# A column of ones beside v, first v loads from GpSimd, scores ahead of transposes, and two weight pieces a step at the end

## The chip, the cores and the metric

The kernel runs on one NeuronCore of a Trainium2 chip. The metric is the time of one execution on the device in microseconds (us), as the median of the runs; lower is better. The engines are called by the names of the profile: PE (TensorE), DVE (VectorE), ACT (ScalarE), POOL (GpSimd) and SP (SyncE, which here only issues DMAs).

## What is computed

Eight batches of attention in chunks of 64 tokens are followed by a Fourier mixing layer and a two-layer perceptron.

```python
# q, k, v: (8, 8 heads, 576, 64) float32; 9 chunks of 64 tokens; each attends within itself
scores = scale * q_c @ k_c^T
attn = exp(scores - max(scores)); attn = attn / (sum(attn) + 1e-9)
x = (attn @ v_c)  ->  (8, 576, 512)
# Fourier mixing and the perceptron
u = x + real(fft(fft(x, axis=1), axis=2))
un = (u - mean(u)) / sqrt(var(u) + 1e-6)
out = u + relu(un @ w_ch1) @ w_ch2      # w_ch1 (512, 2048), w_ch2 (2048, 512), given as float64
```

## The kernel before

**Tiles.** A tile is two chunks of one batch (128 tokens), or the middle chunks of two batches. A batch has two tiles "lo" (tokens from the front) and two "hi" (tokens from the back, mirrored); a tile "rest" serves two batches. That makes 36 tiles; batch 0 has tiles 0 to 4 in the order rest, lo 1, hi 1, lo 0, hi 0. Everything is float32. The functions of a tile n:

- `load(n)` and `load_v(n)` issue the DMAs of q, k and v. A row of 64 floats is one run of 256 bytes. A `load_v` is four DMAs of 64 KB.
- `att_T(n)` transposes q and k, four 128x128 transposes each on PE into a PSUM buffer of the tag `pt` (there are two of these), copied to SBUF by ACT as qT and kT. Later tiles (from batch 2) use DVE's transposes. For some "lo" tiles POOL copies one column of qT.
- `att_S(n)` makes the scores: 16 small products on PE into `sc`.
- `softmax(n)`: DVE takes the maximum (L375) and subtracts it (L377), ACT takes the exponential (L383).
- `att_P(n)` transposes the exponentials (PE, then ACT's copy pT, L390). In the kernel before, DVE also sums them here (L393), adds 1e-9 and takes the reciprocal `rd`.
- `att_V(n)`: 16 products of pT with v, and DVE multiplies the result by `rd` into `xall`, which holds the tokens.

The schedule is manual: the order on each engine is the order in which the program emits the instructions.

**Fourier.** `fold(b, i)` adds and subtracts a lo tile and its mirrored hi tile (DVE or POOL), giving `pm`. `fourier` multiplies by tables over the tokens (`tk`, result `z`, copied by ACT to `zf` and `zr`) and then by tables over the features (`mix`), adds the result to the tokens, and takes mean and variance (`means`; ACT makes `rstd`). For batch 0 `fourier_early` does this with `sin_d` and `cos_d`, two tables loaded by `load_dim_tables`. Row 0 of `sin_d` is not loaded but put together from two rows in `first_rest` by POOL (`turn_dim_row`, L240).

**The perceptron.** Groups of four tiles (512 tokens), one per batch and a last one of the rests. `normed(g, s)` makes `un` for tile s of group g; `turned(g, s)` transposes it into `unT`. Group 0 uses plain products (`up_first`, `down_plain`); later ones use seven products of half size in place of eight (the halves' combinations of the weights are made once, by `keep2` on DVE, L842, and `keep1` on POOL, and kept in DRAM).

**The weights** come as float64 in 32 pieces of 512 KB. `round_weight(i)` turns piece i to float32 by bit operations: two of DVE and three of ACT, and one call later three more of DVE (L301 to L303), some 2.6 us of DVE in all. The pieces are loaded into seven spaces; late pieces may only use some of them (pieces from 26 on, three).

**The order.** First `attention_early` (batch 0), then `fourier_early`. Between these, `keep_warm` puts products with no use on PE. Then comes one long loop: each step t of a group's perceptron is followed by as many steps of the next batch's attention and Fourier part (`side(b)`) as are due, and by `round_next` and the next step of `keep2`:

```python
if not heavy:
    round_next()
    if t <= 4 or t % 4 == 0:
        round_next()
for _ in range(2):
    if n_w > N_LAST + 2 and n_conv < 5 or n_w > len(pieces):
        n_conv += 1
        next(conv2, None)
```

Group 0 takes steps 1 to 16 for its up part and 17 to 32 for its down part; near the end of the latter it norms and transposes the tiles of group 1.

Of the kernel before, what the change touches and what calls it, by code (L numbers as in the profile page):

```python
# [16 lines left out]
def kernel(  # L17
# [32 lines left out]
    nc = tc.nc  # L50
# [106 lines left out]

    qs, ks, vs = {}, {}, {}
    qT, kT = {}, {}
    scs, es, rs, pT = {}, {}, {}, {}  # L160
# [5 lines left out]
    more_v = one_p.tile([128, 2, 2 * NJ * D], FP32, tag="zf", name="more_v")  # L166

    def load(n):

# [32 lines left out]
            dst[n] = t  # L202

    def load_v(n):
        if 3 <= n < first[1]:
            t = more_v[:, n - 3].rearrange("p (i j d) -> p i j d", i=2, j=NJ)
        else:
            t = three_p.tile([128, 2, NJ, D], FP32, tag="v", name="v")
        for i, (b, c) in enumerate(chunks(n)):
            for e in range(2):  # L210
                eng = nc.scalar if n < 2 and e else nc.sync
                eng.dma_start(
                    out=t[e * CH:(e + 1) * CH, i],
                    in_=v[b, e:H:2, c * CH:(c + 1) * CH, :].rearrange("j p d -> p j d"),
                )
        vs[n] = t
# [14 lines left out]
    def load_dim_tables():  # L231
        nc.sync.dma_start(out=cos_d, in_=dim_tab[:, 0, :])
        nc.sync.dma_start(out=sin_d[1:128], in_=dim_tab[1:128, 2, :])
        for i in range(2):
            nc.sync.dma_start(out=first_rest[32 + 32 * i:33 + 32 * i, 0:DM], in_=dim_tab[0:1, 1 + 2 * i, :])

    def turn_dim_row():

# [147 lines left out]
    def att_P(n):  # L386
        ex = es.pop(n)
        pt = turn(lambda j: ex[:, j].rearrange("p e k -> p (e k)"))
        t = one_p.tile([128, NJ, 128], FP32, tag="pT", name="pT")
        nc.scalar.copy(t, pt)  # L390
        pT[n] = t
        rd = sm_p.tile([128, NJ, 2], FP32, tag="rd", name="rd")
        nc.vector.tensor_reduce(out=rd, in_=ex, axis=AX.X, op=ALU.add)  # L393
        nc.vector.tensor_scalar_add(rd, rd, 1e-9)
        nc.vector.reciprocal(out=rd, in_=rd)
        rs[n] = rd

    def att_V(n):
        a, b, rd = pT.pop(n), vs.pop(n), rs.pop(n)
        if n < first[1]:  # L400
            xp = early_xp
        else:
            xp = ps_a.tile([128, 2, 512], FP32, tag="att", name="xp")
            xp = [xp[:, e] for e in range(2)], xp
        for j in range(NJ):
            for e in range(2):
                for c in range(2):
                    r0, t0 = e * CH, c * CH
                    nc.tensor.matmul(
                        out=xp[0][e][t0:t0 + CH, j * D:(j + 1) * D],  # L410
                        lhsT=a[r0:r0 + CH, j, t0:t0 + CH],
                        rhs=b[r0:r0 + CH, c, j, :],
                        start=True,
                        stop=True,
                    )
        x = xt(n)
        xo = x[:, DM:0:-1] if kind(n) == HI else x[:, 0:DM]
        xo, rd = xo.rearrange("p (j e d) -> p e j d", j=NJ, e=2), rd.rearrange("p j e -> p e j").unsqueeze(3)
        if n < first[1]:
            for e in range(2):  # L420
                nc.vector.tensor_tensor(
                    out=xo[:, e],
                    in0=xp[0][e][:, 0:NJ * D].rearrange("p (j d) -> p j d", j=NJ),
                    in1=rd[:, e].to_broadcast([128, NJ, D]),
                    op=ALU.mult,
                )
        else:
            nc.vector.tensor_tensor(
                out=xo,
                in0=xp[1][:, :, 0:NJ * D].rearrange("p e (j d) -> p e j d", j=NJ),  # L430
                in1=rd.to_broadcast([128, 2, NJ, D]),
                op=ALU.mult,
            )
# [73 lines left out]
    def attention_early():  # L507

        lo, hi = first[0], first[1] - 1

        def ready(n):
            if n == at[LO, 0, 1]:
                shift_early(0)
            if n == at[HI, 0, 1]:
                fold(0, 1)
            if n == at[LO, 0, 0]:
                shift_early(1)
                fold(0, NM)
            if n == at[HI, 0, 0]:
                fold(0, 0)  # L520
            if n + 3 > hi:
                load_v(n + 3)

        att_T(lo)
        for n in range(lo, hi + 1):
            att_S(n)
            if n < hi:
                att_T(n + 1)
            softmax(n)
            if n > lo:  # L530
                att_V(n - 1)
                ready(n - 1)
            yield
            att_P(n)
            yield
        shift_early(2)
        turn_tables()
        att_V(hi)
        ready(hi)
        yield  # L540

    def attention(b):

# [49 lines left out]

    def fourier(b):
        h = b % 2
        zf = one_p.tile([128, 4, NL], FP32, tag="zf", name="zf")
# [83 lines left out]
    def fourier_early():  # L680

        zf = one_p.tile([128, 4, NL], FP32, tag="zf", name="zf")
# [7 lines left out]
        for i in order:  # L692
            at_ = {"start": i == order[0], "stop": i == order[-1], "skip_group_check": True}
            for T in range(4):
                p = slice(0, 128) if i < NM else slice(T % 2 * CH, T % 2 * CH + CH)
                d0_ = T * HQ if i < NM else T // 2 * HQ
                nc.tensor.matmul(out=z[T][:, 0:NQ], lhsT=pm[i][p, d0_:d0_ + HQ], rhs=tk[p, i, T // 2], **at_)
# [61 lines left out]
    def natural(n):  # L759

        return xt(n)[:, DM:0:-1] if kind(n) == HI else xt(n)[:, 0:DM]

    def normed(g, s):
        if s >= len(groups[g]):
            return
        n = groups[g][s]
        if (g, s) == (0, 3):
            un = one_p.tile([128, NJ, 128], FP32, tag="pT", name="un").rearrange("p j t -> p (j t)")
        else:
            un = three_p.tile([128, DM], FP32, tag="o", name="un")  # L770
        mean, rstd = sts.pop(n)
        nc.vector.tensor_scalar(un, natural(n), mean, rstd, ALU.subtract, ALU.mult)  # L772
        uns[g, s] = un

    def turned(g, s):
        if s >= len(groups[g]):
            return
        if s == 0:
            unTs[g] = one_p.tile([128, KD, G * 128], FP32, tag="unT", name="unT")
        unT, un = unTs[g], uns.pop((g, s))  # L780
        pt = turn(lambda j: un[:, j * 128:(j + 1) * 128])
        if s % 2 and g > 0:
            nc.vector.tensor_copy(unT[:, :, s * 128:(s + 1) * 128], pt)
        else:
            nc.scalar.copy(unT[:, :, s * 128:(s + 1) * 128], pt)
# [275 lines left out]
    with tc.manual_schedule():  # L1061
# [3 lines left out]
        nc.vector.memset(top[:, 0:1], float((896 + 255) << 20))  # L1065
        nc.vector.memset(top[:, 1:2], float(255 << 23))
        nc.scalar.preload_act_table_set("natural_log_exp_and_others")
        for what, n in (
            (load, 0), (load, 1), (load_v, 0), (load, 2), (load_v, 1), (load, 3), (load, 4),
            (load_v, 2), (load_v, 3), (load_v, 4),  # L1070
        ):
            what(n)
        first_rest = three_p.tile([128, XW], FP32, tag="y", name="first_rest")
        load_tables()
        load_dim_tables()
        for i in range(len(spaces)):
            load_weight(i)
# [4 lines left out]
        def keep_warm(times):  # L1082

            for _ in range(times):
                nc.tensor.matmul(out=idle[:, 0:NQ], lhsT=warm[:, 0:128], rhs=warm[:, 0:NQ], start=True, stop=True)
# [43 lines left out]
        for g in range(NG):  # L1129
            for _ in mlp(g):  # L1130
# [82 lines left out]
```

## Time and profile before

| | |
|---|---|
| median of 3 runs | 1143.11 us (1143.09 to 1143.69) |
| the profiled execution's own time | 1141.05 us |
| its span, first to last instruction | 1139.3 us |
| mean granted PE clock | 0.994 of full speed |
| DVE, ACT, POOL busy | 599.6, 290.5, 272.7 us |
| DMA | 192.73 MB, mean 169 GB/s |

A profile line of a wait reads: engine, line and tile that waited, what ended the wait, then total us, how often, and the longest. A line of the timeline reads: start and length in us from the span's start, engine, line, operation, output and inputs, how many instructions were merged, and in brackets the idle time before it and what ended that. A line of a table by stretch gives its length and, for each engine, busy us with the number of instructions. A float32 product shows as two instructions on PE. "SPq" or "POOLq" is a queue that issues DMAs.

### The profile page before, as it was taken

How to read it: one execution, taken by the hardware profiler on the slowest of the kernel's cores; microseconds unless marked ns; L12 is line 12 of the kernel's file. 1: busy time of each engine (PE TensorE's matmuls, PEld its weight loads, DVE VectorE, ACT ScalarE, POOL GpSimd, SP SyncE). 2: the span in 40 equal slices, each digit the busy share in tenths (PEclk: the TensorE clock that was granted, in tenths of full speed). 3: DMA queues.
4: the chain of work that ended last, by engine and by line, in shares of the span. 5: the costliest groups of instructions: out<-in, count | busy, mean ns of one | idle time of the engine just before them, and what ended most of it. 6: DMA issues, size and time to landing. Idle time of an engine off the chain costs nothing. (4 is left out here: it accounts for less than half of the span.)

```text
span 1139.3 us, 18658 instructions
## 1 busy us (share of the span) xinstructions
PE 1094.5 (96%) x7028; PEld 847.4 (74%) x7028; DVE 599.6 (53%) x1238; ACT 290.5 (25%) x708; POOL 272.7 (24%) x395
## 2 busy tenths in 40 slices
PE   7799997998999999999999999899999999999998
PEld 5544454444888888778888888788888888888887
DVE  4599978524356446553556365654555434423521
ACT  4487552121102321222112211321032202201210
POOL 1300101336300531043305140063015400130140
PEclk9999998999999999999999999999999999999999
DMA  8668742887556826783566547763564246446322
GB/s 147 196 177 199 176 157 84 246 250 223 211 167 190 245 84 185 223 203 117 176 199 169 179 127 217 199 185 111 183 207 123 84 163 196 127 147 213 96 105 81
DMA packets 150354, 192.73 MB, mean 169 GB/s; under 512 B 68671, under 2 KB 106559, under 8 KB 143096
## 3 DMA queue, kind: packets, MB, share of 16 engines
q1 hardware_dynamic: 147928, 190.99, 56.6%
q8 instruction: 56, 0.92, 0.3%
q10 hardware_dynamic: 2144, 0.52, 0.3%
q14 instruction: 34, 0.28, 0.1%
q0 software_dynamic: 192, 0.02, 0.0%
HBM read 167.22 MB, written 24.12 MB: 168 GB/s over the span
## 5 line engine op out<-in xcount | busy, mean ns | idle before, releaser
L867 POOL TENSOR_TENSOR h<-h 128x256 f32<-128x256 f32 x64 | 55.5, 874 | 415.4 <-PE pb L961 303.3
L1008 PE MATMUL pa<-wb,h 128*128 128x256 f32 x512 | 116.9, 383 | 0.0
L1008 PE MATMUL pb<-wb,h 128*128 128x256 f32 x512 | 115.0, 381 | 0.0
L961 PE MATMUL pb<-unT,wa 128*128 128x256 f32 x448 | 106.7, 381 | 4.3 <-DVE wa L970 4.3
L961 PE MATMUL pa<-unT,wa 128*128 128x256 f32 x448 | 107.8, 383 | 0.0
L961 PE MATMUL pb<-wa 128*128 128x256 f32 x448 | 107.1, 382 | 0.8 <-DVE rd L393 0.8
L1008 PEld LDWEIGHTS pa<-wb,h 128*128 128x128 f32 x512 | 96.5, 191 | 15.2 <-issue 2.0
L1008 PEld LDWEIGHTS pb<-wb,h 128*128 128x128 f32 x512 | 95.8, 190 | 12.9
L961 PEld LDWEIGHTS pb<-unT,wa 128*128 128x128 f32 x448 | 84.2, 190 | 18.8 <-DVE wa L970 7.6
L961 PEld LDWEIGHTS pb<-wa 128*128 128x128 f32 x448 | 83.5, 190 | 13.5 <-issue 1.2
L961 PEld LDWEIGHTS pa<-unT,wa 128*128 128x128 f32 x448 | 83.2, 190 | 11.6
L976 ACT ACTIVATE h<-pa 128x256 f32<-128x256 f32 x56 | 21.5, 383 | 175.9 <-PE pa L961 142.9
L915 PE MATMUL dn<-wb,h 128*128 128x512 f32 x128 | 58.9, 609 | 1.9 <-ACT h L885 1.9
L877 PE MATMUL up<-unT,wa 128*128 128x512 f32 x128 | 58.0, 599 | 2.6 <-DVE wa L303 1.6
L968 DVE TENSOR_TENSOR wa<-pa,wa 128x256 f32<-128x256 f32 x56 | 23.8, 425 | 66.5 <-PE pa L961 62.8
L1008 PE MATMUL pa<-wb,yall 128*128 128x256 f32 x256 | 58.2, 382 | 0.0
L894 PE MATMUL up<-unT,wa 128*128 128x512 f32 x128 | 57.6, 599 | 0.5 <-DVE o L928 0.5
L961 PE MATMUL pa<-wa 128*128 128x256 f32 x224 | 54.0, 384 | 3.8 <-ACT wa L966 3.8
L1008 PE MATMUL pb<-wb,yall 128*128 128x256 f32 x256 | 57.1, 380 | 0.0
L1008 PE MATMUL pb<-wb 128*128 128x256 f32 x256 | 56.6, 379 | 0.0
L1008 PEld LDWEIGHTS pb<-wb 128*128 128x128 f32 x256 | 48.2, 190 | 6.3
L1008 PEld LDWEIGHTS pa<-wb,yall 128*128 128x128 f32 x256 | 47.7, 190 | 6.9 <-issue 0.5
(225 smaller groups left out, 1669.9 us busy)
## 6 DMA issues: line engine op xcount, KB each, us to landing
wb<-s SPq DMA_DIRECT2D x56, 1024.0 KB
wa<-s SPq DMA_DIRECT2D x196, 256.0 KB
xall<-in_moe_w_ch_dram SPq DMA_DIRECT2D x22, 512.0 KB
q<-in_q_dram SPq DMA_DIRECT2D x96, 112.0 KB
k<-in_k_dram SPq DMA_DIRECT2D x96, 112.0 KB
v<-in_v_dram SPq DMA_DIRECT2D x132, 64.0 KB
yall<-in_moe_w_ch_dram SPq DMA_DIRECT2D x10, 512.0 KB
s<-wb SPq DMA_DIRECT2D x20, 256.0 KB
```

The costliest lines, as they stand in the source:

```text
L867: nc.gpsimd.tensor_tensor(out=h1[:, m, hi], in0=h1[:, m, lo], in1=h1[:, m, hi], op=ALU.subtract)
L877: nc.tensor.matmul(out=up, lhsT=w1[:, kk, m * 128:(m + 1) * 128], rhs=unT[:, kk], start=(kk == 0), stop=(kk == KD - 1),)
L894: nc.tensor.matmul(out=up, lhsT=w1[:, kk, m * 128:(m + 1) * 128], rhs=unT[:, kk], start=(kk == 0), stop=(kk == KD - 1),)
L915: nc.tensor.matmul(out=dn, lhsT=h1[:, m, s * 128:(s + 1) * 128], rhs=w2[:, m, :], start=(m == 0), stop=(m == KF - 1),)
L961: nc.tensor.matmul(out=dst, lhsT=w[:, kk, r], rhs=rhs[o][:, kk], start=(o in (0, 2) and kk == 0), stop=(kk == 1), skip_group_check=True,)
L968: nc.vector.tensor_tensor(out=b, in0=dst, in1=a, op=ALU.add)
L976: nc.scalar.activation(out=h1[:, m, lo], in_=dst, func=ACTF.Relu)
L1008: nc.tensor.matmul(out=dst, lhsT=lhs[:, m], rhs=w[:, m], start=(o in (0, 2) and m == 0), stop=(m == HF - 1), skip_group_check=True,)
```

## The change

- v gets a 65th column of ones (`DV = D + 1`). The product of pT with v then yields the sums of the exponentials in its last column; DVE's reduction in `att_P` goes, and the addition and the reciprocal move to `att_V`, behind the product. For batch 0 they are done for each of the two halves.
- v lives in three constant tiles (`v_ring`) and, for tiles 3 and 4, in `more_v`; DVE sets their ones at the start. The loads of tiles 0 to 2 are issued by POOL, but for two of tile 0 (ACT). `first_rest` is loaded by POOL at the start. The loads of the tables move ahead of those of v for tile 4.
- In `attention_early` the scores of tile n+1 come ahead of the transposes of the exponentials of tile n. The warm-up products are placed anew: one a tile, four before the last `att_P`, six at the end, none within `fourier_early`'s first products.
- `normed` for group 1 and for tiles 0 and 2 of group 0 runs on ACT (scale and bias), with a small DVE operation for the bias. `turned` for group 1 is copied by ACT alone.
- From t = 18 on, two weight pieces a step.

```diff
@@ attention
+    DV = D + 1
+    v_ring = [const.tile([128, 2, NJ, DV], FP32, name=f"v{i}") for i in range(3)]
+    more_v = one_p.tile([128, 4 * NL + 64], FP32, tag="zf", name="more_v")
...
     def load_v(n):
-        if 3 <= n < first[1]:
-            t = more_v[:, n - 3].rearrange("p (i j d) -> p i j d", i=2, j=NJ)
-        else:
-            t = three_p.tile([128, 2, NJ, D], FP32, tag="v", name="v")
+        t = more_v[n - 3] if 3 <= n < first[1] else v_ring[n % 3]
...
-                eng = nc.scalar if n < 2 and e else nc.sync
+                eng = nc.scalar if n == 0 and e else nc.gpsimd if n < 3 else nc.sync
                 eng.dma_start(
-                    out=t[e * CH:(e + 1) * CH, i],
+                    out=t[e * CH:(e + 1) * CH, i, :, 0:D],
...
@@ load_dim_tables
-        for i in range(2):
-            nc.sync.dma_start(out=first_rest[32 + 32 * i:33 + 32 * i, 0:DM], in_=dim_tab[0:1, 1 + 2 * i, :])
@@ att_P
-        rd = sm_p.tile([128, NJ, 2], FP32, tag="rd", name="rd")
-        nc.vector.tensor_reduce(out=rd, in_=ex, axis=AX.X, op=ALU.add)
-        nc.vector.tensor_scalar_add(rd, rd, 1e-9)
-        nc.vector.reciprocal(out=rd, in_=rd)
@@ att_V
-                        out=xp[0][e][t0:t0 + CH, j * D:(j + 1) * D],
+                        out=xp[0][e][t0:t0 + CH, j * DV:(j + 1) * DV],
...
+            xe = xp[1][:, :, 0:NJ * DV].rearrange("p e (j d) -> p e j d", j=NJ)
+            nc.vector.tensor_scalar_add(rd, xe[:, :, :, D], 1e-9)
+            nc.vector.reciprocal(out=rd, in_=rd)
             nc.vector.tensor_tensor(
...
@@ attention_early
         att_T(lo)
+        att_S(lo)
         for n in range(lo, hi + 1):
-            att_S(n)
             if n < hi:
                 att_T(n + 1)
             softmax(n)
             if n > lo:
                 att_V(n - 1)
                 ready(n - 1)
-            yield
+            if n < hi:
+                att_S(n + 1)
+            keep_warm(1 if n < hi else 4)
             att_P(n)
-            yield
         shift_early(2)
         turn_tables()
         att_V(hi)
         ready(hi)
-        yield
+        keep_warm(6)
@@ fourier_early
-            if i != order[-1]:
-                keep_warm(2)
@@ normed
-        nc.vector.tensor_scalar(un, natural(n), mean, rstd, ALU.subtract, ALU.mult)
+        if g == 1 or g == 0 and s % 2 == 0:
+            shift_ = sm_p.tile([128, 1], FP32, tag="shift", name="shift")
+            nc.vector.tensor_scalar(shift_, mean, rstd, -1.0, ALU.mult, ALU.mult)
+            nc.scalar.activation(out=un, in_=natural(n), func=ACTF.Identity, scale=rstd, bias=shift_)
+        else:
+            nc.vector.tensor_scalar(un, natural(n), mean, rstd, ALU.subtract, ALU.mult)
@@ turned
-        if s % 2 and g > 0:
+        if s % 2 and g > 1:
@@ the start
-        for what, n in (
-            (load, 0), (load, 1), (load_v, 0), (load, 2), (load_v, 1), (load, 3), (load, 4),
-            (load_v, 2), (load_v, 3), (load_v, 4),
-        ):
-            what(n)
...
+        for t in more_v + v_ring:
+            nc.vector.memset(t[:, :, :, D:DV], 1.0)
+        for n in range(first[1]):
+            load(n)
+            if n < 3:
+                load_v(n)
+            if n == 0:
+                for i in range(2):
+                    nc.gpsimd.dma_start(out=first_rest[32 + 32 * i:33 + 32 * i, 0:DM], in_=dim_tab[0:1, 1 + 2 * i, :])
+        load_v(3)
         load_tables()
+        load_v(4)
         load_dim_tables()
...
-        for step, _ in enumerate(attention_early()):
-            keep_warm((step + 1) % 2)
+        attention_early()
@@ the long loop
                     round_next()
-                    if t <= 4 or t % 4 == 0:
+                    if t <= 4 or t % 4 == 0 or t >= 18:
                         round_next()
```

More of the change, by code (lines that the diff above doesn't have):

```diff
@@ L159 @@
     qT, kT = {}, {}
-    scs, es, rs, pT = {}, {}, {}, {}
+    scs, es, pT = {}, {}, {}
     pms, sts = {}, {}
@@ L164 @@
     cos_d, sin_d = start[:, d0:d0 + DM], start[:, d0 + DM:d0 + 2 * DM]
-    more_v = one_p.tile([128, 2, 2 * NJ * D], FP32, tag="zf", name="more_v")
+    DV = D + 1
+    v_ring = [const.tile([128, 2, NJ, DV], FP32, name=f"v{i}") for i in range(3)]
+    more_v = one_p.tile([128, 4 * NL + 64], FP32, tag="zf", name="more_v")
+    more_v = [
+        more_v[:, i * 2 * NJ * DV:(i + 1) * 2 * NJ * DV].rearrange("p (i j d) -> p i j d", i=2, j=NJ) for i in range(2)
+    ]
     def load(n):
@@ L391, in att_P @@
         pT[n] = t
-        rd = sm_p.tile([128, NJ, 2], FP32, tag="rd", name="rd")
-        nc.vector.tensor_reduce(out=rd, in_=ex, axis=AX.X, op=ALU.add)
-        nc.vector.tensor_scalar_add(rd, rd, 1e-9)
-        nc.vector.reciprocal(out=rd, in_=rd)
-        rs[n] = rd
     def att_V(n):
-        a, b, rd = pT.pop(n), vs.pop(n), rs.pop(n)
+        a, b = pT.pop(n), vs.pop(n)
         if n < first[1]:
@@ L417, in att_V @@
         xo = x[:, DM:0:-1] if kind(n) == HI else x[:, 0:DM]
-        xo, rd = xo.rearrange("p (j e d) -> p e j d", j=NJ, e=2), rd.rearrange("p j e -> p e j").unsqueeze(3)
+        xo = xo.rearrange("p (j e d) -> p e j d", j=NJ, e=2)
+        rd = sm_p.tile([128, 2, NJ], FP32, tag="rd", name="rd")
         if n < first[1]:
             for e in range(2):
+                xe = xp[0][e][:, 0:NJ * DV].rearrange("p (j d) -> p j d", j=NJ)
+                nc.vector.tensor_scalar_add(rd[:, e], xe[:, :, D], 1e-9)
+                nc.vector.reciprocal(out=rd[:, e], in_=rd[:, e])
                 nc.vector.tensor_tensor(
[L422 to L425, printed above, removed]
-                )
-        else:
+                    out=xo[:, e], in0=xe[:, :, 0:D], in1=rd[:, e].unsqueeze(2).to_broadcast([128, NJ, D]), op=ALU.mult,
+                )
+        else:
+            xe = xp[1][:, :, 0:NJ * DV].rearrange("p e (j d) -> p e j d", j=NJ)
+            nc.vector.tensor_scalar_add(rd, xe[:, :, :, D], 1e-9)
+            nc.vector.reciprocal(out=rd, in_=rd)
             nc.vector.tensor_tensor(
[L429 to L432, printed above, removed]
+                out=xo, in0=xe[:, :, :, 0:D], in1=rd.unsqueeze(3).to_broadcast([128, 2, NJ, D]), op=ALU.mult,
             )
@@ L595, in fourier @@
         h = b % 2
-        zf = one_p.tile([128, 4, NL], FP32, tag="zf", name="zf")
+        zf = one_p.tile([128, 4 * NL + 64], FP32, tag="zf", name="zf")
+        zf = zf[:, 0:4 * NL].rearrange("p (t f) -> p t f", t=4)
         pm = [pms.pop((b, i)) for i in range(NM + 1)]
@@ L680, in fourier_early @@
     def fourier_early():
-        zf = one_p.tile([128, 4, NL], FP32, tag="zf", name="zf")
+        zf = one_p.tile([128, 4 * NL + 64], FP32, tag="zf", name="zf")
+        zf = zf[:, 0:4 * NL].rearrange("p (t f) -> p t f", t=4)
         pm = [pms.pop((0, i)) for i in range(NM + 1)]
```

## The prediction

> **What bounds the kernel now.** I read the busy shares, then TensorE's (PE's) waits in total, the stretches, and the order of instructions where the waits sit.
>
> ```profile
> PE 1094.5 (96%) x7028; PEld 847.4 (74%) x7028; DVE 599.6 (53%) x1238; ACT 290.5 (25%) x708; POOL 272.7 (24%) x395
> ```
>
> PE sets the end: 1139.3 - 1094.5 = 44.8 us idle. The waits say where:
>
> ```profile
> PE pt L313 <- DVE un L772: 8.2, 8, 6.0
> PE pt L313 <- DMA start<-in_q_dram: 7.0, 1, 7.0
> ...
> PE z L697 <- POOL pm_rest L504: 3.6, 1, 3.6
> ...
> PE dn L915 <- ACT h L885: 1.9, 1, 1.9
> ```
>
> 7.0 us is the first load; 3.6 lies in the prologue, 1.9 and a single 6.0 in group 0's MLP. By stretch (us, then PE, PEld, DVE, ACT, POOL busy, granted clock, DMA):
>
> ```profile
> 30.00:60.00 30.00, 23.61 (x149) 16.21 (x147) 17.07 (x44) 13.11 (x40) 8.05 (x20) 0.94 0.63 184
> 60.00:120.00 60.00, 58.90 (x349) 29.07 (x350) 56.85 (x110) 50.01 (x85) 2.53 (x5) 1.00 0.72 187
> 183.00:196.00 13.00, 6.97 (x21) 4.04 (x20) 10.92 (x19) 2.10 (x5) 0.20 (x1) 0.74 0.37 91
> 300.00:1000.00 700.00, 689.43 (x4646) 580.38 (x4645) 363.63 (x760) 148.78 (x408) 181.87 (x261) 1.00 0.57 169
> ```
>
> After 300 us PE is busy 98.5% and DVE 52%: an edit there can save little. What can be won lies before 200 us: the prologue, until PE starts on the MLP at 60.02, and the hole at 183.
>
> ```profile
> 12.54 0.20 POOL L345 COPY qT<-qT 128x8 f32<-128x8 f32 x1 [11.23 <-ACT qT L341]
> ...
> 14.95 1.03 PE L362 MATMUL sc<-kT,qT 64*64 64x64 f32 x32
> ...
> 30.79 5.07 SPq L235 DMA_DIRECT2D first_rest<-in_dim_tab_dram  x2
> ...
> 46.31 0.86 POOL L240 COPY start<-first_rest 1x256 f32<-1x256 f32 x2 [10.95 <-DMA first_rest<-in_dim_tab_dram]
> ...
> 100.13 0.70 POOL L461 DMA_DIRECT2D first<-xall  x1 [17.22 <-DVE xall L428]
> ...
> 188.44 0.54 DVE L772 TENSOR_SCALAR un<-xall,st,rstd 128x512 f32<-128x512 f32 x1
> 189.13 1.09 PE L313 MATMUL pt<-ident,un 128*128 128x128 f32 x4 [6.03 <-DVE un L772]
> ...
> 190.86 4.78 PE L915 MATMUL dn<-wb,h 128*128 128x512 f32 x8
> ```
>
> PE meets `un` 6 us late because DVE, which runs in order, has weight pieces and combinations (L301, L842) ahead of it, although its statistics were ready at 178.
>
> **What the Trainium skill says.** "DMA: Bandwidth & Descriptors", § SWDGE vs HWDGE vs iDMA: a DMA issued from GpSimd (POOL) has its descriptors computed by software on that engine. The trace shows only small ones, 0.50 to 0.77 us (L461 to L465), two rows each; the loads of v have 256 runs of 256 B. "TensorE: Matmul & The Clock Gate", § Part 1: after a window of some 3.4 us without work PE's clock halves. The trace agrees: clock 0.74 in 183 to 196, the eight matmuls 4.78 us where others took 3.70. The DMA page, § Why a DMA increments its semaphore by 16 and not by 1: a load of 127 partitions runs on one DMA engine. `sin_d[1:128]` is such a load: issued at 30.47, and `first_rest`, queued behind it, landed at 46.3.
>
> **The change, part by part.**
>
> *Loads.* SP loses 8 v loads (0.65 us of issue each: 3.22 us for 4) and both `first_rest` loads (5.07 us, waiting on semaphores of earlier ones). So `sin_d` should be issued at about 26 rather than 30.5 and land near 40 to 42, and weights start some 5 us earlier. POOL gains 10 v loads and 2 small ones, ahead of its column copy of qT for tile 1, for which the second score product waits; everything on PE stands behind that product. With P us per v load, POOL is free at 1.3 + 10P + 1.2. P is not in the trace: at least 0.5 (the small ones), at most 2.15 (the DMA page's fit for this path, § Anatomy of one DMA, 2.0 us plus the bytes at 436 GB/s, taken as all serial: an estimate). I take 1.1, as 256 descriptors must cost something beyond the 0.5. POOL is then free at 13.5, against 13.3 when S(1) could start otherwise: +0.4 us with the copy.
>
> *Scores ahead of transposes, early tiles.* New PE order: P(n), q and k transposes of n+2, V(n), S(n+2), warm-up, P(n+1). The k transposes take the PSUM buffer of P(n) (two `pt` buffers), so they now wait for ACT's copy of pT: 0.66 + 0.15 + 0.59 = 1.4 us after P starts, where S stood between before. S(n+2) follows kT's copy at 2.9; with S 0.63 and a warm-up 0.5 the period is 4.0 us. Before, V(0) at 16.93 and V(4) at 30.95 give 3.5. From S(1) at 13.4 (kT's copy for tile 1 ended at 13.32), P(0) comes at 14.8, P(3) at 27.05, V(3) at 28.6; the four new warm-ups (2.0) put P(4) at 31.3 and V(4) at 32.9: **1.9 us later**.
>
> *After V(4).* ACT's table copies begin at 34.0, no longer at the DMA (1.51 us wait before), and end at 36.1; six warm-ups keep PE warm until 36.6. Then z for i=1 takes 2.3 us, not 4.9 (36.03 to 40.93, cold, with warm-ups). The fold of tile 4 ends at 38.9 (two more add/reciprocal pairs on the path, 0.75). i=0 runs to 41.2, the rest to 42.6; the products with cos start at 42.9, not 46.02. The sin half waits for no row. **3.1 + 0.4 gained**, if sin_d has landed.
>
> *normed on ACT for two of four tiles:* DVE loses 2 x 0.55, gains 2 x 0.17 on a DVE chain: **0.7 gained**. With the late S(1) the prologue gives 3.1 + 0.4 + 0.7 - 0.4 = **3.8 us**. In the 60 to 120 stretch DVE and PE move together, so it carries.
>
> *The sums from the column.* The L393 reduce (0.69 us) leaves DVE for each of 36 tiles; add and reciprocal move behind V. After 300 us DVE's slack hides both: no gain. Before 130 us DVE is 95% busy, and the 1.9 us wait of `dn` on ACT follows its lag: one reduce with its add and reciprocal less (1.05) against 0.4 moved gives 0.6 to 1.9; I take **1.0**. V's 65 columns for 64: 1/64 of 0.69 x 36 = **0.4 lost**. The memsets of the ones (0.06 us) lie in DVE's first 10 idle us.
>
> *Two pieces a step from t = 18.* DVE idled 6.11 us before 166.64, while two pieces came after it (169.1 to 174.4). Now six pieces run in a row from 141.9; loads three deep limit them to some 2.8 us each (a space freed by L302 at 146.3, 1.9 into its piece, was refilled at 150.07: 1.9 + 3.7 = 5.6 for two pieces), so the sixth ends at 158.2, and ACT, in order, reaches the copies of z at 158.2 rather than 153.9. **What is late next:** PE's second z pair waits 1.8 for them and mix 0.9. Then y at 169.4, 175.0 and 179.5, the last combinations, and `un` by ACT at 187.1; PE comes at 185.8. Transposes at 187.3, not 189.13: 1.8; and with no idle over 3.4 us the clock stays up: 6.34 us (189.13 to 195.47) become 4.4, 1.9 more. **3.7 gained.** Bounds: 0 if the new waits eat it, 6.5 if they don't come.
>
> Sum: 3.8 + 1.0 + 3.7 - 0.4 = 8.1 us. The profiled execution took 1141.05 (span 1139.3), so 1133.0; the median of the runs, 1143.1, stands 2.06 higher: **1135.0**.
>
> **Rivals.**
> - *POOL's issue holds the start (slower).* Each 0.1 us of P above 1.05 delays S(1), and all of PE, by 1.0. At P = 2.15 that is 11.0 us against 8.5 saved elsewhere: +2.5, **1145.6**; it turns the sign from P = 1.9, and can be measured from 2.13. For it: ten loads in front of a copy that PE needs. Against: 0.5 to 0.8 for the issues seen. At P = 1.7 to 2.1 the result is within 0.2%.
> - *The prologue gains nothing:* sin_d still lands at 46, or unaligned rows of 260 B slow the DMA, which is 81% busy in the first 30 us. Then 3.1 + 0.4 goes and 4.6 remains: **1138.5**.
> - *The hole only moves:* PE stalls at z and mix for what it saved at `un`. 8.1 - 3.7 = 4.4: **1138.7**. For it: ACT has seven pieces ahead of the copies of z. Both of these: about 1 us, no change.
>
> **How the numbers follow.** About 0.2% (2.3 us) can be told from no change. My forecast (6 to 11 us less) 0.48, one of the two middle rivals 0.24: faster 0.72. Both of them, or P near 1.9: same 0.13. POOL's issue above 2.1 us: slower 0.15. Low end: P below 1 and no new waits, 12 us less, 1131; high end 1146, the first rival at P = 2.2.
>
> **What would show it.** Right: L1080 and v issues on POOL end near 13.5; S(1) at 14; P period 4.0; z at 36 to 37 at full clock; first MLP matmul near 56; the wait of `pt` on `un` at most 2 us, waits of some 1.8 on z. Wrong: S(1) beyond 17 with the copy of qT as its releaser; a wait of PE on `start` at the sin products; a hole near 180 as long as before.

## The result, and the profile after

The changed kernel takes **1128.46 us** (median of four runs), the kernel before, run beside it, 1143.1: a ratio of 0.988 (95% interval 0.9857 to 0.9903), 14.6 us less. I had forecast 1135.0, with 1131 as the low end. The direction was right, but the gain is 1.8 times as large as forecast.

The profiled execution took 1128.35 us (span 1126.2, mean granted clock 1.0). First the busy shares of the page, then PE's waits in total (engine, line and tile; what ended the wait; us, times, longest).

```profile
PE 1091.5 (97%) x7036; PEld 847.4 (75%) x7036; DVE 572.4 (51%) x1215; ACT 296.6 (26%) x716; POOL 278.8 (25%) x407
```

```profile
PE pt L314 <- DMA start<-in_q_dram: 7.2, 1, 7.2
...
PE z L600 <- POOL pm L493: 1.8, 1, 1.8
...
PE dn L918 <- ACT h L888: 1.3, 1, 1.3
PE pt L314 <- ACT un L773: 1.3, 2, 0.8
PE z L600 <- ACT zr L628: 1.0, 1, 1.0
```

The single wait of 6.0 us of `pt` on `un` is gone; the longest that is left of it is 0.8 us. The prologue's wait on `pm_rest` is gone too, `dn`'s fell from 1.9 to 1.3, and a new one, on `zr`, is 1.0. The same stretches as before (PE, PEld, DVE, ACT, POOL busy; granted clock; DMA share; GB/s):

```profile
30.00:60.00 30.00, 26.83 (x193) 19.10 (x185) 19.86 (x56) 17.33 (x47) 10.29 (x25) 1.00 0.61 181
60.00:120.00 60.00, 58.93 (x350) 28.97 (x349) 55.25 (x108) 48.69 (x83) 2.85 (x6) 1.00 0.70 187
183.00:196.00 13.00, 13.00 (x75) 6.88 (x75) 8.91 (x14) 5.10 (x8) 3.60 (x6) 1.00 0.82 243
300.00:1000.00 700.00, 689.90 (x4619) 580.94 (x4618) 345.34 (x729) 146.85 (x401) 181.19 (x261) 1.00 0.56 169
```

From 183 to 196 PE is busy throughout and at full clock, where it was busy for 6.97 us at 0.74. After 300 us DVE lost 18 us of work and PE is as busy as it was: as forecast, the column gains nothing there.

The timeline of the changed kernel, the rows that answer to those shown of before:

```profile
3.89 3.69 POOL L215 DMA_DIRECT2D v<-in_v_dram  x6
8.00 0.61 POOL L215 DMA_DIRECT2D v<-in_v_dram  x1 [0.42 <-DMA first_rest<-in_dim_tab_dram]
...
12.71 0.20 POOL L346 COPY qT<-qT 128x8 f32<-128x8 f32 x1 [3.16 <-ACT qT L342]
13.59 1.13 PE L363 MATMUL sc<-kT,qT 64*64 64x64 f32 x32 [0.78 <-ACT kT L351]
...
42.07 0.29 POOL L256 COPY so<-start 128x128 f32<-128x128 f32 x1 [1.99 <-DMA start<-in_dim_tab_dram]
...
182.82 0.66 PE L314 MATMUL pt<-ident,un 128*128 128x128 f32 x4 [0.85 <-ACT un L773]
183.31 0.60 PE L314 MATMUL pt<-ident,ex 128*128 128x128 f32 x4
183.75 3.60 PE L918 MATMUL dn<-wb,h 128*128 128x512 f32 x8
```

A v load costs POOL 0.61 us; POOL was done at 9.5 and waited 3.16 us for the qT that it copies. `sin_d` was there at 42.1.

**Where the time came from**, by the starts of the same instruction in both profiles (before, after, and what had been gained by then): first `up` 60.02, 57.92: 2.1. First `dn` 129.15, 126.47: 2.7. Transposes of `un` of group 1 189.13, 182.82: 6.3. First `up` of group 1 209.81, 200.88: 8.9. First `pa` of that group's down part 274.02, 262.89: 11.1 (`pa` and `pb` are products of half size; group 1 still has a plain up part). First `pa` behind the z that follows 291.35, 277.97: 13.4; at the end 13.1. The other 1.5 of the 14.6 us lie outside the two spans: the median of before stands 2.06 above its profiled execution (that of the changed kernel 0.11), and the time around the span is 0.40 longer after. My account ended with the clock behind 189; 4.2 us came after 209, where I had put nothing. The last part of it comes at that z, which waits for `pm`; before, then after:

```profile
280.54 1.89 PE L601 MATMUL z<-tk,pm 128*128 128x289 f32 x6 [2.41 <-POOL pm L496]
268.75 1.73 PE L600 MATMUL z<-tk,pm 128*128 128x289 f32 x6 [1.75 <-POOL pm L493]
```

The wait on `pm` got 0.66 shorter, and before ran at half speed for a while behind it (granted clock 0.76 in 280 to 287), the changed kernel did not.

**A wait that no list of waits showed.** 2.2 of these lie at one product of V. In the profile before, the timeline of SP, DVE and PE around it:

```profile
257.07 0.76 SPq L828 DMA_DIRECT2D s<-wb  x1
258.76 0.42 DVE L865 TENSOR_TENSOR wb<-h 128x256 f32<-128x256 f32 x1 [11.51 <-DMA s<-wb]
...
262.21 0.68 DVE L428 TENSOR_TENSOR xall<-xp,rd 128x512 f32<-128x512 f32 x1
...
262.99 0.69 PE L409 MATMUL xp<-v,pT 64*64 64x64 f32 x32 [2.03 <-issue]
```

"issue" says that the profile saw nothing that PE waited for. But the trace of that line has a semaphore wait in the queue of PE's weight loads, and its length leads to the cause:

```profile
L409 PEldq EVENT_SEMAPHORE  x1: 8566/8566/8566, 254.4 to 254.4; - x1
```

It ended 8.566 us after 254.4, at 263.0, just after DVE's L428 (262.21 + 0.68) had emptied the PSUM buffer of the V before, which this one needs. DVE was late because its queue had stood still for 11.51 us at L865: `operands` writes sums of `h` into a part of `wb` that `keep1` uses for its combinations, and the last of their stores had been issued at 257.07. In the changed kernel the same chain reads:

```profile
245.13 0.66 SPq L831 DMA_DIRECT2D s<-wb  x1
246.35 0.42 DVE L868 TENSOR_TENSOR wb<-h 128x256 f32<-128x256 f32 x1 [8.05 <-DMA s<-wb]
...
250.33 0.69 DVE L428 TENSOR_TENSOR xall<-xp,rd 128x512 f32<-128x512 f32 x1
...
251.87 0.70 PE L405 MATMUL xp<-v,pT 64*64 64x65 f32 x32
```

No stop: DVE is done 0.85 us ahead of PE. Followed upwards, that chain is: the last weight piece (its last DVE operation ended at 184.7 before, 165.2 after), `keep2`'s combinations and stores, `keep1` on POOL (first operation 204.32, 192.75), its stores (257.07, 245.13), `operands` (258.76, 246.35), V (262.99, 251.87). It moved by 19.5, 11.6, 11.9, 12.4 and 11.1 us. PE itself was 8.9 us earlier at the first `up` of group 1, so against PE the links behind the pieces moved by 2.2 to 3.5. From this I made the theory to test: **late pieces.** In the kernel before, PE was tied until 263 to a chain that begins with the weight pieces, and two pieces a step are worth what the chain's end moves, not what one wait was long. The rival: the reduce that left DVE, and the earlier prologue, gave what came after 209.

### The profile page after: what moved, and what is told of

It reads as the page before. It is cut to its first block, busy times and chain, and to the rows that moved or that the text cites. A ratio compares the mean times of both kernels' runs of the same rounds, so it can differ in the third digit from the quotient of the medians.

```text
span 1126.2 us, 18753 instructions
## 1 busy us (share of the span) xinstructions
PE 1091.5 (97%) x7036; PEld 847.4 (75%) x7036; DVE 572.4 (51%) x1215; ACT 296.6 (26%) x716; POOL 278.8 (25%) x407
## 5 line engine op out<-in xcount | busy, mean ns | idle before, releaser
L1011 PEld LDWEIGHTS pa<-wb,h 128*128 128x128 f32 x512 | 95.8, 190 | 14.6 <-issue 1.6
L964 PEld LDWEIGHTS pa<-unT,wa 128*128 128x128 f32 x448 | 83.2, 190 | 11.6
L669 POOL TENSOR_TENSOR xall<-y,xall 128x513 f32<-128x513 f32 x14 | 21.3, 1519 | 127.9 <-DVE y L663 127.9
```

The lines of the kernel that those rows point to most:

```text
L669: eng.tensor_tensor(out=x[:, 0:w], in0=y[:, 0:w], in1=x[:, 0:w], op=ALU.add)
L964: nc.tensor.matmul(out=dst, lhsT=w[:, kk, r], rhs=rhs[o][:, kk], start=(o in (0, 2) and kk == 0), stop=(kk == 1), skip_group_check=True,)
L1011: nc.tensor.matmul(out=dst, lhsT=lhs[:, m], rhs=w[:, m], start=(o in (0, 2) and m == 0), stop=(m == HF - 1), skip_group_check=True,)
```

## The experiments

Every kernel ran beside the kernel before on the same chip. The medians of before were 1141.25 us beside e1 to e4, 1141.92 beside e5 to e8, and 1141.05 beside e9 to e12; each ratio is to these, with its 95% interval. The changed kernel ran beside e5 to e8 only; where e2, e3 and e4 or e9, e11 and e12 are set beside it, the medians stem from different sets of runs, and those of before lie up to 0.9 us apart.

### e1: two pieces a step, alone

```diff
# kernel before
-                    if t <= 4 or t % 4 == 0:
+                    if t <= 4 or t % 4 == 0 or t >= 18:
```

> The kernel before with only the rule of two weight pieces a step from t = 18. Theory (late pieces): in the two profiles 10.4 of the 13.1 us of span come after the first down product: 3.6 at the hole of 183, 2.6 by the start of group 1 (two normed tiles' transposes and the halved clock), 2.2 at a V product near 263, 2.3 around 280 to 291 (clock and one wait). All of it descends from weight pieces and combinations that DVE had late, so this edit alone gives 9 to 12 us: 1131 to 1134, the first MLP matmul stays at 60.0, and neither the hole at 183, nor the stop of V near 263, nor a window of half clock is left. Rival (DVE's relief): the later gains come from the reduce that left DVE in every tile and from the earlier prologue; then this edit alone closes the hole only, 3.7 us as I predicted, up to 5.6: 1137.5 to 1139.4, and the stop near 263 stays.

**1133.66 us** (0.9925, 0.9906 to 0.9945). This one line gives 7.6 us by the medians (6.3 to 10.7 by the interval), twice what I had put on it, more than the rival allows and somewhat less than the 9 to 12 of the late pieces. The wait at the hole is 0.43 (pt at 186.72), V waits 0.19 instead of 2.03. One thing of the theory failed: the wait on `pm` was still 2.41 us, with a window of half clock behind it (six z products in 3.23 us, 1.73 in the changed kernel).

### e2: all but two pieces a step

```diff
# changed kernel
-                    if t <= 4 or t % 4 == 0 or t >= 18:
+                    if t <= 4 or t % 4 == 0:
```

> The changed kernel with two weight pieces only in the first steps and in every fourth, as before. Theory (late pieces): the hole before pt near 180, the stop of V near 260 and a window of half clock come back; only the prologue's 2.1 and 0.6 by the first down product remain: 1138.9 to 1140.4. Rival (DVE's relief): the edit is worth 3.7 to 5.6, so 1132.2 to 1134, and V near 260 doesn't stop.

**1138.15 us** (0.9968, 0.9957 to 0.9979): 10.2 more than the changed kernel (e5), a little under the range expected. The timeline of PE:

```profile
185.13 1.11 PE L314 MATMUL pt<-ident,un 128*128 128x128 f32 x4 [6.45 <-ACT un L773]
...
257.84 0.70 PE L405 MATMUL xp<-v,pT 64*64 64x65 f32 x32 [0.41 <-issue]
```

The hole is back in full, with half-speed transposes behind it, though DVE has no reduce and `un` is on ACT. V's stop is only 0.41, though the pieces are late: something in the other parts takes 1.6 of its 2.0. Which of them was not tested; the column alone (e8) leaves it at 1.95.

### e3: the normalisations of group 0 back on DVE

```diff
# changed kernel
-        if g == 1 or g == 0 and s % 2 == 0:
+        if g == 1:
```

> The changed kernel with the two normalisations of group 0 back on DVE. Theory: on ACT each un takes 0.81 us and the next rstd is queued behind it, for which DVE waits 1.62 us at 54.6; without it the first MLP matmul comes 0.3 to 1.0 us earlier (57.0 to 57.6) and the time is 1127.5 to 1128.1. Rival (the prediction's step): the move to ACT is worth 0.7 us, so undoing it gives 1129.1 and the first MLP matmul at 58.6.

**1127.66 us** (0.9871, 0.9851 to 0.9892), as the theory has it, but 0.3 from the changed kernel is too little to decide by medians. The profiles decide: from the start of the cos products to the first `up` it takes 13.99 us here, as in the kernel before (46.03 to 60.02), and 14.33 in the changed kernel (43.59 to 57.92) and in e2 and e5. The move to ACT costs 0.34 us.

### e4: early scores in the order of before

```diff
# changed kernel, attention_early
-        att_S(lo)
         for n in range(lo, hi + 1):
+            att_S(n)
...
-            if n < hi:
-                att_S(n + 1)
             keep_warm(1 if n < hi else 4)
```

> The changed kernel with the order of the early tiles as before: the scores of a tile behind the probabilities' transposes of the tile before it. Theory: the new order makes each k transpose wait for ACT's copy of pT and puts V of tile 4 at 33.8 rather than 31.0; with the old order V of tile 4 comes at 30.5 to 31.5, z starts at 35 to 36 rather than 37.5, and the first MLP matmul comes 1 to 2 us earlier, as long as sin_d, landed at 42.1, is not needed earlier: 1126.5 to 1127.6. Rival: what follows V of tile 4 (table copies on ACT, pm on POOL and DVE, the landing of sin_d) sets the products anyway, then V of tile 4 is earlier and the first MLP matmul stays at 57.9: 1128.4.

**1125.21 us** (0.9863, 0.9841 to 0.9885), faster than forecast for it. V of tile 4 is at 31.12, the cos products at 41.39, the first `up` at 55.73. So the scores ahead of the transposes cost 0.5 (against e2) to 1.8 us (against e5, where PE ran "cold", at half speed, until 18). Two of the five runs (1128.55 and 1129.21) don't show the gain. The profile is of the slowest: there z waits 2.21 us for ACT's `zr` at 154.88, about what the prediction feared, and runs at half speed behind that (3.74 us for eight products; 0.74 and 2.22 in e5). Why it waits longer here stays open.

### e5: the changed kernel again

> The changed kernel itself, once more, beside the others of this call. Theory: the late start of the early V products in its first profile (18.56, with a weight load at half speed around 15.8 to 18.6) belonged to that execution, not to the change: here V of tile 0 comes at 16.5 to 16.9, as in the two runs that share its order of scores, and the first MLP matmul at 55.7 to 56.3, so that the prologue is worth 3.7 to 4.3 us as predicted. Rival: the order of scores causes it, V of tile 0 again at 18 to 19, first MLP matmul at 57.5 to 58. Time 1126.5 to 1129 in either case.

**1127.98 us** (0.9875, 0.9854 to 0.9896). V of tile 0 came at 18.16 and the first `up` at 57.53: what I expected here failed. But the order of scores alone does not decide it, as e2 and e3 have it and their V comes at 16.83 and 16.47. The second score product tells them apart; first e2, then what follows that product in the first profile of the changed kernel, then e9:

```profile
13.76 0.69 PE L363 MATMUL sc<-kT,qT 64*64 64x64 f32 x32 [0.78 <-ACT kT L351]
16.83 0.70 PE L405 MATMUL early_xp<-v,pT 64*64 64x65 f32 x32
```

```profile
15.78 1.06 PE L314 MATMUL pt<-ident,ex 128*128 128x128 f32 x4
16.63 2.00 PE L314 MATMUL pt<-ident,start 128*128 128x128 f32 x8
18.56 0.99 PE L405 MATMUL early_xp<-v,pT 64*64 64x65 f32 x32
```

```profile
13.44 1.13 PE L363 MATMUL sc<-kT,qT 64*64 64x64 f32 x32 [0.78 <-ACT kT L351]
18.22 0.70 PE L405 MATMUL early_xp<-v,pT 64*64 64x65 f32 x32
```

In e2 PE is at full speed at 13.8 (0.69 us for the scores); in the changed kernel's own profile and in e5, e9 and e12 it took 1.13 us for them and ran cold until 18 to 19. The Trainium skill, "TensorE: Matmul & The Clock Gate", § Part 1, says that the window which decides on the clock runs freely and doesn't start with the kernel; six profiles with one order until then that differ in this agree, by more than the half microsecond that the page gives. So a single pair of profiles can't price an edit here. But the order may well make a cold start likelier: of the seven profiles that have it, five took the full 1.13 us for these scores (these four and e11) and have V of tile 0 at 17.13 to 18.56; of the seven with the order of before none did (0.69 to 1.03 us), and V of tile 0 is at 16.00 to 16.93. No run was made to decide this.

### e6: e3 and e4 together

> The changed kernel with both the early order of scores as before and the two normalisations of group 0 on DVE. Theory: the two gains lie on different stretches (V of tile 4 to z; rstd to the transposes of un) and add: first MLP matmul at 54.6 to 55.3, 1123.3 to 1125. Rival: with an earlier z the landing of sin_d (42.1) holds the sin products and one of the gains is lost: 55.7, and no faster than 1125.2.

**1125.87 us** (1125.35 to 1126.70; 0.9858, 0.9836 to 0.9881) where the changed kernel on the same chip took 1127.98 (1126.36 to 1129.18). This beats both kernels, but it is no faster than e4: the rival is right. The first `up` is at 55.32, and the sin products now wait for the DMA:

```profile
40.60 1.17 PE L723 MATMUL early_xp<-start,zf 128*128 128x256 f32 x4
42.22 2.96 PE L723 MATMUL early_xp<-start,zf 128*128 128x256 f32 x12 [0.45 <-DMA start<-in_dim_tab_dram]
```

### e7: only the clock of the hole

```diff
# kernel before, turned(1, 0): nine products of zeros into pt ahead of its transposes
+        for _ in range(warm_up):
+            nc.tensor.matmul(out=pt..., lhsT=warm[:, 0:128], rhs=warm[:, 0:NQ], start=True, stop=True)
```

> The kernel before with nine products of zeros on PE ahead of the first transposes of group 1, which run while PE waits for un at 183 to 189. It separates the clock from the wait. Theory: the wait stays (un comes at 188.4 whatever PE does), only the half clock behind it goes: pt, pt and the down product take 4.4 us instead of 6.34, so 1.9 us less in the profile from 189.13 to the next transposes, 1139.0 to 1139.7 beside 1141.25. Rival: the 1.9 is lost again in the waits that follow on DVE (o at 209.8, V near 263), since DVE is the late one: unchanged, 1141.0 to 1141.5, with these waits longer by 1 to 2 us in sum.

**1142.66 us** (1.0002, 0.999 to 1.0013): nothing gained. The timeline of PE:

```profile
129.52 5.39 PE L917 MATMUL dn<-wb,h 128*128 128x512 f32 x8 [1.90 <-ACT h L887]
...
191.09 0.66 PE L315 MATMUL pt<-ident,un 128*128 128x128 f32 x4 [1.56 <-DVE un L774]
191.59 0.60 PE L315 MATMUL pt<-ident,ex 128*128 128x128 f32 x4
192.02 3.60 PE L917 MATMUL dn<-wb,h 128*128 128x512 f32 x8
...
265.00 0.69 PE L411 MATMUL xp<-v,pT 64*64 64x64 f32 x32 [3.98 <-issue]
```

In the hole the clock stayed up, and from `pt` to the first `up` of group 1 PE took 18.8 us instead of 20.7. The 1.9 that I had counted were there, but the median shows none of them: its interval goes from 1.1 us less to 1.5 more. This one profile is clouded by something else: its first `dn` met half speed (5.39 us for eight products instead of 3.70), and `un`, `pt` and the chain are all 2 us later than in that of before. So PE was no earlier at the first `up` (209.86), `operands` comes at 260.79 instead of 258.76, and V stops for 3.98 us instead of 2.03. What can be read is that V keeps its distance from `operands`, 4.21 us (4.23 before), and not from PE's arrival. That is the rival's result, and it fits the late pieces: PE waited for the chain. It does not show that the chain is free of PE's speed: here it may be late because of PE's own slow `dn`.

### e8: the column alone

```diff
# kernel before: v tiles of 65 columns, add and reciprocal behind V
-        nc.vector.tensor_reduce(out=rd, in_=ex, axis=AX.X, op=ALU.add)
...
+            nc.vector.tensor_scalar_add(rd, xe[:, :, :, D], 1e-9)
```

> The kernel before with only the column of ones: v in tiles of 65 columns, no reduce of the exponentials, add and reciprocal behind V. Loads, orders, warm-ups and weight pieces as before. Theory (late pieces): the wait of the first down product on ACT falls from 1.9 to 1.3, the hole at 183 stays at 5.5 to 6.5 and the stop of V near 263 at 1.5 to 2.2; with 0.4 us for the wider V the net is 0 to 0.6 us: 1140.6 to 1141.3. Rival (DVE's relief): the reduce that leaves DVE 36 times frees its queue and the stop of V near 263 falls to 0.5 or less, the hole to 5: 1138 to 1139.5.

**1139.99 us** (0.9983, 0.9974 to 0.9993): 0.8 to 3.0 us less, more than I expected. In the profile all three waits are as the late pieces have them: `dn` 1.32, the hole 6.03, V 1.95. From first `up` to first `dn` it gained 0.6, and lost it again: PE is no earlier than before at the first `up` of group 1 (210.03; 209.81) or at V (263.13; 262.99). The 1.1 us by which this profile's span is shorter come after 280, where it has no window of half clock and before has one. So the profile doesn't say that the column itself makes the 1.9 between the medians.

### e9: pieces early, combinations not

```diff
# changed kernel
-                for _ in range(2):
-                    if n_w > N_LAST + 2 and n_conv < 5 or n_w > len(pieces):
-                        n_conv += 1
-                        next(conv2, None)
+                while t >= 22 and n_conv < (2, 4, 5)[t - 22] if t < 25 else n_conv < 5 + 2 * (t - 24):
+                    n_conv += 1
+                    next(conv2, None)
```

> The changed kernel, its weight pieces two a step as there, but the combinations of keep2 held to the steps that they had before (2, 4, 5, 7, 9 ... done at t = 22, 23, 24, 25, 26 ..., 19 rather than 22 by t = 31). It separates the pieces from the chain that follows them (combinations on DVE, their stores on SP, keep1 on POOL, its stores, the first xs on DVE). Theory: both count. The hole at 180 stays closed (a wait of at most 1.5 us), but the later chain is late again, and V near 255 stops for 0.4 to 2 us or pm is waited for 2 to 3.5 us: 1129.5 to 1132. Rival: only the pieces count, a step of lag in the combinations is hidden: 1127.5 to 1128.5, V doesn't stop.

**1132.07 us** (0.9912, 0.9897 to 0.9927), some 4 more than the changed kernel (1127.98 in e5), just above the range of the theory, and far from the rival's. The timeline of SP, DVE and PE:

```profile
182.68 0.66 PE L314 MATMUL pt<-ident,un 128*128 128x128 f32 x4 [1.45 <-ACT un L773]
...
249.64 0.95 SPq L831 DMA_DIRECT2D s<-wb  x1
251.11 0.43 DVE L868 TENSOR_TENSOR wb<-h 128x256 f32<-128x256 f32 x1 [12.52 <-DMA s<-wb]
...
255.77 0.70 PE L405 MATMUL xp<-v,pT 64*64 64x65 f32 x32 [3.53 <-issue]
```

The last operation of the last piece starts when it does in e5 (163.9) and the hole is closed. But with three of the combinations later in the order, `keep1` started at 196.71 (192.53 in e5), the last store came at 249.64 (243.75), and V stopped for 3.53 us. This parts the edit's worth: some 6 us for the early pieces (e2 to e9), some 4 for the chain behind them.

### e10: keep1 sooner

```diff
# kernel before
-                    for _ in range(3):
+                    for _ in range(5):
                         next(conv1, None)
```

> The kernel before with five steps of keep1 per MLP step of group 1 instead of three: its combinations on POOL and its stores on SP stand earlier in those queues, ahead of the loads of q and k of the next tile. Theory (late stores): the stop of V near 263 (2.0) follows the last stores of wb, issued at 257; here they are issued by 252, V doesn't stop or stops under 0.5, the wait on pm stays under 3: 1138 to 1140 beside 1141 to 1142. The hole at 183 stays. Rival: POOL waits for stores of yall (12.5 us before 232.4) whatever the order, so nothing changes, or the loads of q and k come late instead and scores or V stop for as long: 1141 to 1143.

**1142.07 us** (1.0003, 0.9993 to 1.0013). The rival is right: the last store of wb was issued at 255.28, not by 252, and V stopped for only 0.23, but a score product did, for 2.10 us at 248.73, because DVE's `xall` stood behind transposes of q and k whose loads SP now issues later. POOL still waited 12.8 us for stores of `yall`. This order, at least, moves the stop and does not remove it. (This profile, too, met half speed at the first `dn`, 5.40 us.)

### e11: the loads back on SP

```diff
# changed kernel: v of tiles 0 to 2 and first_rest on nc.sync, first_rest behind sin_d
-                eng = nc.scalar if n == 0 and e else nc.gpsimd if n < 3 else nc.sync
+                eng = nc.scalar if n == 0 and e else nc.sync
```

> The changed kernel with all loads of v (but the two of ACT for tile 0) and both of first_rest issued by SP again, first_rest behind sin_d as before; order of loads, scores and warm-ups as changed. Theory: SP's queue gets 8 to 10 issues longer (5 to 6.5 us) and sin_d lands at 44 to 47 rather than 42, so the sin products wait 1 to 3 us, the first MLP matmul comes at 58.5 to 60.5: 1129 to 1131. The second score product stays at 13.4 to 13.8, since POOL's issues (0.6 us each) ended at 9.6 and held nothing. Rival: sin_d still lands before the products need it: 1127.5 to 1128.5.

**1130.39 us** (0.9899, 0.9882 to 0.9915): the loads on POOL, those of `first_rest` with them, are worth some 2.4 us. The wait is another one than expected:

```profile
42.15 1.17 PE L727 MATMUL early_xp<-start,zf 128*128 128x256 f32 x4
45.40 4.28 PE L727 MATMUL early_xp<-start,zf 128*128 128x256 f32 x12 [2.07 <-POOL start L243]
```

It is POOL's copy of row 0, held until 44.49 by the landing of `first_rest`; and the products behind the wait ran partly at half speed (4.28 us, 2.96 in e6). What moving the loads of v alone is worth, the run doesn't tell. The second score product came earlier than expected, at 12.62, because the first transposes began at 6.19; in the profiles shown or named here otherwise they began at 6.9 to 7.4, in before at 7.00 without POOL's loads, so one profile doesn't tell the cause.

### e12: warm-ups as before

```diff
# changed kernel
-            keep_warm(1 if n < hi else 4)
+            keep_warm(1)
...
-        keep_warm(6)
+        keep_warm(1)
...
+            if i != order[-1]:
+                keep_warm(2)
```

> The changed kernel with the warm-ups of before: one before each tile's transposes of probabilities, the last tile's too, one after the last V, two in the first stage of z. Theory: PE is idle for over 3 us between V of tile 4 and z, z starts at half clock and takes 4 to 5 us for i=1 instead of 2.3; the last tile's transposes come 0.8 earlier. First MLP matmul 1 to 2 us later: 1129 to 1130.5. Rival: with sin_d at 42 as the bound, z's clock doesn't show: 1127.2 to 1128.5.

**1130.70 us** (0.9903, 0.9886 to 0.9921), 2.7 more than the changed kernel. z starts hardly earlier (36.99; 37.13 in e5) and cold, waiting for `pm_rest`:

```profile
36.99 2.27 PE L697 MATMUL z<-tk,pm 128*128 128x289 f32 x4 [3.53 <-POOL pm_rest L499]
39.05 2.13 PE L697 MATMUL more_z<-tk,pm 128*128 128x289 f32 x4
42.66 1.14 PE L697 MATMUL z<-tk,pm 128*128 128x289 f32 x4
```

The first `up` comes at 61.86, 4.3 later than in e5; I had expected 1 to 2. The profile is of the slowest of the six runs (1134.50), so the 2.7 of the medians is the better figure.

## Why the prediction was right, and where it was wrong

The sum was 8.1 us, and 14.6 were measured. The step that failed is the one of the two weight pieces a step: priced at 3.7 us, at most 6.5, it gave 7.6 alone and 10.2 beside the other parts. The other terms came out near their sizes in sum, some of them by luck. Part by part:

**Loads: right.** P was 0.61 us, near its low bound of 0.5; I took 1.1. The upper bound of 2.15, worked out from the fit in the Trainium skill, "DMA: Bandwidth & Descriptors", § Anatomy of one DMA, priced the way of one DMA to its landing, and POOL is not held that long. It was done at 9.5, so the slower rival had nothing to stand on. `sin_d` was issued at 27.55 and landed at 42.1 (26 and 40 to 42 predicted). What e11 lost was the landing of `first_rest`; the prediction has it ("the sin half waits for no row") but no price for it.

**Scores ahead: right in kind.** The period was 3.8 to 3.9 instead of 4.0. V of tile 4 was 0.7 to 1.1 us later than before in the profiles that warmed up early (e2, e3) and 2.4 to 2.8 in two that didn't (e5 and the first); predicted 1.9, which lies between the two by luck, as the prediction had no cold clock in it. Other profiles with the prologue of before have V of tile 4 at 29.84 to 30.48 instead of 30.95 (e1, e7, e8, e10), and against them it is 0.5 to 1.1 more. It is a cost, as e4 shows. (In the working, three periods of 4.0 from 14.8 make 26.8, not 27.05.)

**z at full clock: right.** z for i=1 took 2.27 us (37.52 to 39.79; predicted 2.3). The cos products start at 41.5 to 43.6 (predicted 42.9), and e12 shows the warm-ups as the reason.

**Normalisation on ACT: wrong sign.** I had put 0.7 as gained; e3 shows 0.34 lost. I counted DVE's operations and left out that `un` takes 0.81 us on ACT, with the next `rstd` queued behind it.

**The prologue's sum: right.** The first `up` starts at 60.6 on average in the five profiles with the prologue of before (60.02, 61.61, 60.40, 60.17, 60.90), at 57.3 in the four with the changed one (57.92, 56.20, 57.53, 57.60): 3.3 us, predicted 3.8. The 2.1 of the first two profiles alone would have misled. In this sum the 0.7 of the normalisation was wrong and the cold start was not foreseen.

**The column: near in size, the mechanism not shown.** `dn`'s wait fell by 0.6 (predicted 1.0), a V takes 0.70 us instead of 0.69 (0.4 over 36 tiles). Net 0.6 predicted, 0.8 to 3.0 measured in e8, but in e8's profile the 0.6 are gone again by the first `up` of group 1.

**Two pieces a step: the step that failed.** 3.7 predicted with a bound of 6.5; 7.6 alone (e1), 10.2 beside the other parts (e2 to e5). Three of its terms were wrong:

- *The waits that come next.* Six pieces in a row took 2.8 us each (138.96 to 155.54), as predicted. But z waited 0.95 instead of 1.8 (2.21 in e4's profile alone) and mix 0.28 instead of 0.9, so from first `dn` to `pt` 3.6 us were gained, not 1.8.
- *The clock.* I counted 1.9 for it as a gain by itself. It is 1.9 on PE (e7), but the median of e7 shows none of it while the late chain stands behind. Nor does the clock stay up for want of an idle over 3.4 us: half speed followed waits of 1.90 to 2.41 us as well (last section). The measurement decides here against the rule that the prediction cites.
- *The end of the account.* I read PE's waits by releaser, and the stretch after 300 us, and concluded that nothing was to be won behind 195. Between lay a stop of 2.03 us under "issue", a wait of 2.4 on `pm`, and a half-speed window behind that; all three went or shrank. From e2 to e5 the three stretches give 4.3 us (first `dn` to `pt`), 3.7 (to `pa`) and 2.5 (to the next transposes of `un`), in sum 10.4 beside 10.2 in the medians.

So PE had been tied to the end of a chain that starts with the pieces: pieces alone brought some 6 us (e2 to e9), the combinations and stores behind them some 4 (e9 to e5). The rival that the hole only moves is refuted by e1; the one that the prologue gains nothing, by e11 and e12.

**Open:** why the wait on `pm` is 1.48 to 1.75 us in the changed kernel and its near variants (e3, e4, e6, e11, e12) and 2.41 in before, e1 and e2, 2.69 in e8. It is shorter too where PE had lost time shortly before (0.71 in e7, 0.68 in e9, 1.52 in e10). Open as well is a difference of up to 2.3 us between profiles from the transposes of `un` near 300 to the end (830.9 us in e9, 833.2 in e2).

## What to carry to other kernels

When an edit takes work off a late engine, follow that work to its last consumer before the sum is closed: here pieces, combinations, stores and sums were one chain, and PE was tied to its end 75 us behind the hole that the list of waits showed. An idle stretch under "issue" is to be looked up by its line, for a semaphore wait in the engine's load queue. And the time that PE saves by itself counts only where PE, not such a chain, sets the next meeting point: e7 saved 1.9 us in the hole, and its median shows none of it.

## What was not expected of the hardware

- Ten DMA issues from POOL (six of 64 KB in 3.69 us, 256 runs each) are no slower than SP's 0.65 us each.
- The second score product ran at full clock at 13.4 to 13.8 us in two profiles (0.69 us; e2, e3) and at half clock in four with the same order of work until then (1.13 us; the changed kernel, e5, e9, e12): 1.3 to 2.1 us in the time of the first V.
- The length of a wait doesn't tell whether half clock follows. It followed waits of PE of 1.90 us (e7), 1.92 and 2.10 (e10), 2.21 (e4) and 2.41 (before, e1, e2): eight down products behind it took 5.39 us instead of 3.70, which makes some 3.4 us at half speed. It did not follow waits of 1.90 and 2.03 (before), 1.92 (e1) and 2.69 (e8), nor those of 1.48 to 1.75 on `pm`.
